# Ordering VectorE's work in bundles 1 to 3 of a convolution and channel-mix kernel, and parting one cast between ScalarE and VectorE

## Chip, cores and metric

The kernel runs on one core of a Trainium2 chip. The metric is the device time of one execution in microseconds, as the median of several runs. The core has five engines with a queue each, which meet at semaphores: TensorE (PE, matmuls), VectorE (DVE), ScalarE (ACT), GpSimd (POOL) and SyncE (SP, which here only starts transfers). Each engine works through its own instructions in the order in which the program has them.

## The reference

The input x has 8 sequences of 4160 positions and 192 channels. A causal convolution with 7 taps comes first; its taps are a softmax over `weight`, one row for each of 8 heads of 24 channels. Its result y feeds a channel mix:

```
y_prev = y shifted by one position
xk = mu_k * y + (1 - mu_k) * y_prev
xr = mu_r * y + (1 - mu_r) * y_prev
k  = relu(xk @ w_k)                  # 192 -> 1024
v  = (k * k) @ w_v                   # 1024 -> 192
r  = sigmoid(xr @ w_r)               # 192 -> 192
out = r * v
```

## The kernel before, and what sets its order

**Tiles.** Two sequences are worked on together, so there are four pairs. Positions of a pair are cut into steps of 512 (the first pair begins and ends with a step of 256). For a step, K = xk @ w_k makes 1024 rows of k for 512 positions of two sequences; a slot is one eighth of that, a PSUM tile `ps_k` of 128 x 1024 fp32. ScalarE takes it to SBUF as `k_sb` (ReLU, `k_relu`), VectorE squares it into `k2` (`k_square`), and TensorE uses `k2` for V (`v`, `v_rows`). Four slots in a row are a bundle. Slots 0 to 3 (bundle 0) belong to step 0, slots 4 to 11 (bundles 1 and 2) to step 1, slots 12 to 19 (bundles 3 and 4) to step 2. So the third step is step 2, and the second and third bundle are bundles 1 and 2.

**Mixing.** VectorE makes xk and xr of a step from the difference d = y - y_prev (`diff`, L528): three scalings by mu, one for each third of the channels (`scale`, L559), and one addition of y_prev (`add_y`, L565). xk must be there before the first slot of its step, xr before the R of that step (`r`, L642), which runs a bundle or two later.

**Convolution.** Positions are grouped; the first groups of pair 0 are made on TensorE and stay on the chip. Group 3, the fourth, is convolved by `conv_full` in bundle 2 into two PSUM tiles `ps_c`, cast to `y` by `conv_out` (L431), turned by 15 transposes in bundle 3 (`tr`, L494) and copied into `yT` by VectorE (L503). The second of the two tiles needs two casts, of 320 and of 640 elements in each partition, since its heads cross a border between thirds of the channels. Groups 4 and 5 go through `conv_tiles` (L317) from bundle 3 on.

**What sets the order.** The program is written out by hand, bundle by bundle: `bundle_first`, `bundle_second`, `bundle_third` for bundles 0 to 2 and `bundle_rest` behind them. Pieces of mixing are put into tables (`mix_a`, `mix_b`, `mix_c`, `late`) under a bundle's number by `at`, and `run` calls them at fixed places in a bundle. Every call appends to the queue of its engine, so the order of calls is the order on each engine. Two supplies of buffers tie the engines together:

- `ring`: four PSUM buffers for every kind of tile (`ps_k`, `ps_r`, `ps_v`, `ps_c`, `ps_t`). A matmul into a new tile waits until the reader of the buffer's last tile is done.
- `four`: four buffers for `k_sb`. The ReLU of slot n waits for the square of slot n - 4.

Which free buffer of the ring a tile gets is chosen when the program is built, and can change when other work moves.

In bundle 2 TensorE does K of slots 8, 9 and 10, R of step 0, V of step 0, the two tiles of group 3 and K of slot 11. In bundle 3 it does K of slots 12 and 13, the transposes of group 3, two convolution tiles of group 4, K of slot 14, R of step 1, half of a V, K of slot 15, two more tiles, and the other half of V.

Of the kernel before, what the change touches and what calls it, by code (L numbers as in the profile page):

```python
# [14 lines left out]
def kernel(  # L15
# [11 lines left out]
    nc = tc.nc  # L27
# [36 lines left out]
    for p in range(NPAIR):  # L64
# [5 lines left out]
        for L in sizes:  # L70
            ns = L * NF // STEP
# [7 lines left out]
    bundles, bundle_of = [], {}  # L79
    n = 0  # L80
# [100 lines left out]
    n = groups[0][2] * 2 * D  # L181
# [190 lines left out]
    def conv_units(g):  # L372

        return [((0, 1), (6, 7)), ((2, 3), (4, 5))]
# [39 lines left out]
        c0 = YC + groups[g][1] + b0 * BLK  # L414
        copy(out=yTs[0][:, c, c0 : c0 + (b1 - b0) * BLK], in_=o[:, 0 : (b1 - b0) * BLK])  # L415

    def conv_out(g, c, copy):

        nb = groups[g][2]
        unit = conv_units(g)[c]  # L420
        w = G * len(unit[0])
        ps = conv_ps.pop((g, c))[:BLK, :, :]
        y = ys[g][:BLK, :, :]
        parts = []
        for hs in unit:
            c0, c1 = hs[0] * G, (hs[-1] + 1) * G
            cuts = [c0] + [a for a in range(Q, D, Q) if c0 < a < c1] + [c1]
            parts.append(sorted((b - a, a - c0, a // Q * 2 * Q + a % Q) for a, b in zip(cuts, cuts[1:])))
        for (n, s0, d0), (m, s1, d1) in zip(*parts):
            assert n == m and d1 > d0  # L430
            copy(  # L431
                out=bass.AP(
                    tensor=y.tensor,
                    offset=y.offset + d0,
                    ap=[y.ap[0], [d1 - d0, 2], [2 * D, nb], [Q, 2], [1, n]],
                ),
                in_=bass.AP(
                    tensor=ps.tensor,
                    offset=ps.offset + s0,
                    ap=[ps.ap[0], [BANK + s1 - s0, 2], [2 * w, nb], [w, 2], [1, n]],  # L440
                ),
            )
# [126 lines left out]
    def k_mm(n, cs=range(NC)):  # L569


        s, j = slots[n]
        L = steps[s][2]
        xk = xks[s]
        if cs[0] == 0 and n not in k_ps:
            k_ps[n] = ring.tile([P, 2, BANK], FP32, tag="k", name="ps_k")
        ps = k_ps[n]
        nf = STEP // L

        for c in cs:  # L580
            for f in range(nf):
                fs = slice((j * nf + f) * P, (j * nf + f + 1) * P)
                for i in range(2):
                    r = slice(i * Q, (i + 1) * Q)
                    nc.tensor.matmul(  # L585
                        out=ps[:, i, f * L : (f + 1) * L],
                        lhsT=wk[r, c, fs],
                        rhs=xk[r, c, :L],
                        start=c == 0 and f == 0,
                        stop=c == NC - 1 and f == nf - 1,  # L590
                    )

    def k_relu(n):
        ps = k_ps.pop(n)
        k_sb = four.tile([P, 2 * STEP], BF16, tag="k_sb", name="k_sb")
        k_sbs[n] = k_sb
        nc.scalar.activation(out=k_sb, in_=ps.rearrange("p a b -> p (a b)"), func=AF.Relu)  # L597

    def k_square(n):
        s, j = slots[n]  # L600
        L = steps[s][2]
        k_sb = k_sbs.pop(n)
        if j == 0:
            k2s[s] = three.tile([P, NF, 2 * STEP], BF16, tag="k2", name="k2")
        nf = STEP // L
        i = k_sb
        o = k2s[s][:, j, :]
        if nf > 1:
            i = k_sb.rearrange("p (b f t) -> p f b t", b=2, f=nf)
            o = k2s[s][:, j * nf : (j + 1) * nf, 0 : 2 * L].rearrange("p f (b t) -> p f b t", b=2)  # L610
        nc.vector.tensor_tensor(out=o, in0=i, in1=i, op=ALU.mult)  # L611
# [74 lines left out]
    def v_out(s, j):  # L686
        p, t0, L, _, _ = steps[s]
        o_sb = four.tile([P, 4, D], FP32, tag="o_sb", name="o_sb")
        nc.vector.tensor_tensor(  # L689
            out=o_sb.rearrange("p (b t) d -> p b (t d)", b=2),  # L690
            in0=v_ps.pop((s, j)),
            in1=r_sbs.pop((s, j)),
            op=ALU.mult,
        )
        for st in range(2):
            c = t0 + 2 * j * P
            nc.sync.dma_start(
                out=out[2 * p + st, c : c + 2 * P, :].rearrange("(m p) d -> p m d", p=P),
                in_=o_sb[:, 2 * st : 2 * st + 2, :],
            )  # L700
# [24 lines left out]
    early, rq, rs, xt, mix_a, mix_b, mix_c, vq, late = ({} for _ in range(9))  # L725

    def at(table, b, fn, *a):
        table.setdefault(b, []).append((fn, a))

    for g, (p, base, nb, fb, on_pe) in enumerate(groups):  # L730
# [10 lines left out]
        if g in sparse:  # L741
            at(late, max(fb - 5, xs[-1] + 2), y_read, g, slice(0, 1), 2)
            at(late, fb - 2, y_read, g, slice(1, 2), 2)
            b, b1 = {6: (3, 5), 7: (9, 10), 8: (16, 17)}.get(g, (fb - 19, fb - 16))
# [16 lines left out]
    for s, (p, t0, L, n0, ns) in enumerate(steps):  # L761
        fb = first_bundle[s]
        if s == 0:
            at(mix_a, 1, mix, s, 1)
            continue
        if s == 1:
            at(mix_b, 1, scale, s, 1, 0, 1)
            at(late, 2, scale, s, 1, 2)
            at(late, 2, add_y, s, 1)
        else:  # L770
            if s == 2:
                at(mix_c, 1, diff, s)
            elif s == 4:
                at(mix_b, fb - 1, diff, s)
            else:
                at(mix_c, fb - 2, diff, s)
            at(mix_b if s == 4 else mix_a, fb - 1, scale, s, 0, 0)
            at(mix_b, fb - 1, scale, s, 0, 1, 2)
            at(mix_c, fb - 1, add_y, s, 0)
            if s == 2:  # L780
                at(mix_a, fb, scale, s, 1, 0)
                at(mix_b, fb, scale, s, 1, 1)
            else:
                at(mix_c, fb - 1, scale, s, 1, 0)
                at(mix_a, fb, scale, s, 1, 1)
            at(mix_b, fb, scale, s, 1, 2)
            at(mix_b, fb, add_y, s, 1)
        if s == LAST - 1 or s < LAST and steps[s + 1][0] > p:
            at(late, fb - 1, keep_tail, p)
    for s, j, vb in quads:  # L790
        b = vb - (s == LAST)
# [7 lines left out]
    def run(table, b, part=slice(None)):  # L799
        for fn, a in table.get(b, [])[part]:  # L800
            fn(*a)
# [165 lines left out]
    def bundle_third(b, ns):  # L967

        quad = vq[b][0]
        first, second = xt[b - 1]  # L970
        for n in bundles[b - 1][2:]:
            k_square(n)
        run(mix_a, b)
        for n in ns[:3]:
            k_mm(n)
            k_relu(n)
        k_square(ns[0])
        run(rq, b)
        run(rs, b)
        v(*quad)  # L980
        conv_full(*first)
        conv_full(*second)
        conv_out(*first, nc.scalar.copy)
        k_square(ns[1])
        run(mix_b, b)
        k_mm(ns[3])
        k_relu(ns[3])
        conv_out(*second, nc.scalar.copy)
        v_out(*quad)
        run(mix_c, b)  # L990
        run(late, b)

# [55 lines left out]
```

## Time and profile before

| what | value |
|---|---|
| median of 3 runs | 412.27 us |
| lowest and highest run | 411.48, 414.23 us |
| profiled execution, its own time | 410.83 us |
| its span (first to last instruction) | 409.0 us |
| outside of the span | 1.83 us |
| instructions | 17463 |
| granted TensorE clock, mean | 1.000 |

The profile is of one execution, taken by the hardware. Its start times count from the first instruction. A row of a timeline merges equal instructions that follow each other; what stands in brackets is how long the engine was idle before it and what ended that idle time. In a row such as `xk<-d,mu` the tile that is written stands on the left. Numbers such as `k_sb_516`, in the lists of instructions below, tell the buffers' tiles apart: `k_sb_602`, `656`, `675`, `684`, `693`, `766`, `792` and `801` belong to slots 6 to 13, `ps_k_857` to slot 14.

### The profile page before, as it was taken

The numbers are of one execution on the slowest core, as the hardware profiler recorded it, in microseconds if no ns is written. First come the engines' busy times: TensorE is split into PE (matmuls) and PEld (weight loads), VectorE is DVE, ScalarE is ACT, GpSimd is POOL, SyncE is SP. The second block draws the span as 40 slices with busy tenths as digits, with TensorE's granted clock in tenths as the row PEclk, the third lists the DMA queues.
The fourth block names the chain that finished last, engine by engine and source line by source line (L and its number), as shares of the span: only waits on it lengthen the run. The fifth ranks groups of instructions, "written<-read, shape, count | busy, mean of one in ns | idle before, by whom it ended". The sixth has DMA issues, their size and how long they took to land.

```text
span 409.0 us, 17463 instructions
## 1 busy us (share of the span) xinstructions
PE 400.1 (98%) x7695; PEld 301.4 (74%) x7696; DVE 370.7 (91%) x672; ACT 354.3 (87%) x426; POOL 57.2 (14%) x91
## 2 busy tenths in 40 slices
PE   7889999999999999999999999999999999999996
PEld 5557777777877777777777777777777778777795
DVE  5989899998999999999999999999999899999973
ACT  6889989989888989988898998889899877877781
POOL 8632202300240202004020022000000000000000
PEclk9999999999999999999999999999999999999999
DMA  9999999989399998789995997977523846221223
GB/s 148 185 202 204 189 203 208 214 241 187 92 197 265 195 209 131 156 192 197 202 160 135 234 169 133 169 192 195 128 79 94 218 123 157 81 73 46 80 79 117
DMA packets 138955, 66.23 MB, mean 162 GB/s; under 512 B 89356, under 2 KB 138880, under 8 KB 138880
## 3 DMA queue, kind: packets, MB, share of 16 engines
q1 hardware_dynamic: 95536, 48.20, 46.9%
q0 software_dynamic: 42544, 16.36, 35.1%
q8 instruction: 60, 0.98, 1.0%
q10 hardware_dynamic: 800, 0.57, 0.5%
q14 instruction: 15, 0.12, 0.1%
HBM read 33.29 MB, written 36.86 MB: 172 GB/s over the span
## 4 chain that ended last, share of the span: by engine, by line
PE 95%; DMA 2%; POOL 1%; ACT 1%; issue 0%; DVE 0%; POOLq 0%
PE ps_k L585 41%; PE ps_v L673 41%; PE ps_r L642 8%; PE ps_c L362 2%; PE ps_v L625 2%; DMA wk<-in_moe_w_k_dram 2%; ACT k_sb L597 0%; PE ps_c L317 0%; POOL wk L224 0%; POOL xb L152 0%; PE ps_t L405 0%; PE ps_c L387 0%; ACT y L431 0%; POOL tap L258 0%; DVE o_sb L709 0%
## 5 line engine op out<-in xcount | busy, mean ns | idle before, releaser
L597 ACT ACTIVATE k_sb<-ps_k 128x1024 bf16<-128x1024 f32 x260 | 253.4, 1039 | 35.4 <-PE ps_k L585 34.6
L611 DVE TENSOR_TENSOR k<-k_sb 128x1024 bf16<-128x1024 bf16 x260 | 173.5, 688 | 24.9 <-ACT k_sb L597 24.7
L585 PE MATMUL ps_k<-xk,wk 64*128 64x512 bf16 (+1 forms) x1632 | 191.6, 367 | 2.5 <-DMA wk<-in_moe_w_k_dram 1.6
L673 PE MATMUL ps_v<-wv,k 64*128 64x192 bf16 x3968 | 185.3, 243 | 0.0
L673 PEld LDWEIGHTS <-k 64*128 64x128 bf16 x3968 | 165.7, 94 | 11.8 <-issue 4.4
L585 PEld LDWEIGHTS <-wk 64*128 64x128 bf16 x1632 | 83.3, 94 | 58.9 <-DMA wk<-in_moe_w_k_dram 2.1
L689 DVE TENSOR_TENSOR o_sb<-ps_v,r_sb 128x768 f32<-128x768 f32 x64 | 60.9, 951 | 2.6 <-issue 2.4
L152 POOL DMA_DIRECT2D xb<-in_x_dram x62 | 43.5, 708 | 132.2 <-DVE xb L111 60.1
L653 ACT ACTIVATE r_sb<-ps_r 128x768 bf16<-128x768 f32 x65 | 53.5, 824 | 7.4 <-PE ps_v L673 5.1
L335 ACT CAST y<-ps_c 128x960 bf16<-128x960 f32 (+2 forms) x84 | 52.7, 710 | 0.0
L642 PEld LDWEIGHTS <-xr 64*128 64x128 bf16 x780 | 34.9, 94 | 14.5 <-issue 0.5
L642 PE MATMUL ps_r<-wr,xr 64*128 64x192 bf16 x780 | 43.3, 243 | 0.0
L559 DVE TENSOR_SCALAR xr<-d,mu 128x512 bf16<-128x512 bf16 (+1 forms) x102 | 35.4, 351 | 0.0
L559 DVE TENSOR_SCALAR xk<-d,mu 128x512 bf16<-128x512 bf16 (+1 forms) x99 | 32.6, 358 | 0.1
L528 DVE TENSOR_TENSOR d<-yT 128x1536 bf16<-128x1536 bf16 (+4 forms) x36 | 31.2, 866 | 1.1 <-ACT yT L415 1.1
L565 DVE TENSOR_TENSOR xr<-xr,yT 128x1536 bf16<-128x1536 bf16 (+1 forms) x33 | 31.1, 941 | 1.1
L565 DVE TENSOR_TENSOR xk<-xk,yT 128x1536 bf16<-128x1536 bf16 (+3 forms) x33 | 30.5, 923 | 0.1
L512 POOL COPY y_tail<-yT 128x195 bf16<-128x195 bf16 x4 | 3.1, 764 | 88.8 <-DMA yT<-y_dram 88.8
L362 PEld LDWEIGHTS <-toe 32*32 32x32 bf16 x768 | 4.9, 87 | 10.3 <-issue 8.7
L362 PE MATMUL ps_c<-xb,toe 32*32 32x240 bf16 x768 | 10.8, 266 | 0.0
L125 POOL MEMSET xb<- 32x384 bf16 x3 | 1.2, 409 | 66.6 <-DVE xb L123 66.6
L625 PE MATMUL ps_v<-wv,k 128*128 128x192 bf16 x96 | 8.4, 246 | 0.0
(60 smaller groups left out, 62.7 us busy)
## 6 DMA issues: line engine op xcount, KB each, us to landing
out_dram<-o_sb SPq DMA_DIRECT2D x128, 192.0 KB
xb<-in_x_dram POOLq DMA_DIRECT2D x52, 240.0 KB, 8.1
y_dram<-y SPq DMA_DIRECT2D x48, 195.0 KB
y_dram<-y SPq DMA_DIRECT2D x8, 210.0 KB
xb<-in_x_dram POOLq DMA_DIRECT2D x6, 228.0 KB, 5.1
xb<-in_x_dram POOLq DMA_DIRECT2D x4, 192.0 KB, 6.3
wk<-in_moe_w_k_dram POOLq DMA_DIRECT2D x4, 192.0 KB, 6.4
wv<-in_moe_w_v_dram POOLq DMA_DIRECT2D x1, 384.0 KB, 8.4
```

The costliest lines, as they stand in the source:

```text
L152: nc.gpsimd.dma_start(out=xb[q0 : q0 + rows, lo:hi, s, :], in_=bass.AP(tensor=x.tensor, offset=x.offset + (b * S + t0 + lo * step) * D, ap ...
L335: nc.scalar.copy(out=bass.AP(tensor=y.tensor, offset=y.offset + d, ap=[y.ap[0], [m * 2 * D, 2], [2 * D, m], [Q, 2], [1, b - a]],), in_=bas ...
L528: nc.vector.tensor_tensor(out=shaped(s, diffs[s][:, cs, :L]), in0=y_of(s, cs, 1), in1=y_of(s, cs, 0), op=ALU.subtract)
L559: nc.vector.tensor_scalar(out=t[:, c, :L], in0=diffs[s][:, c, :L], scalar1=mu[:, i, c : c + 1], scalar2=None, op0=ALU.mult)
L565: nc.vector.tensor_tensor(out=o, in0=o, in1=y_of(s, sl, 0), op=ALU.add)
L585: nc.tensor.matmul(out=ps[:, i, f * L : (f + 1) * L], lhsT=wk[r, c, fs], rhs=xk[r, c, :L], start=c == 0 and f == 0, stop=c == NC - 1 and f ...
L597: nc.scalar.activation(out=k_sb, in_=ps.rearrange("p a b -> p (a b)"), func=AF.Relu)
L611: nc.vector.tensor_tensor(out=o, in0=i, in1=i, op=ALU.mult)
L642: nc.tensor.matmul(out=ps[:, i, k * D : (k + 1) * D], lhsT=xr[q, c, ts], rhs=wr[q, c, :], start=c == 0, stop=c == NC - 1,)
L653: nc.scalar.activation(out=r_sbs[s, j], in_=r_ps.pop((s, j))[:, :, 0 : 2 * D], func=AF.Sigmoid)
L673: nc.tensor.matmul(out=v_ps[s, j][:, bank, k * D : (k + 1) * D], lhsT=k2s[s][q, f, t * P : (t + 1) * P], rhs=wv[q, f, :], start=half == 0 ...
L689: nc.vector.tensor_tensor(out=o_sb.rearrange("p (b t) d -> p b (t d)", b=2), in0=v_ps.pop((s, j)), in1=r_sbs.pop((s, j)), op=ALU.mult,)
```

## The change

Four things change, all in bundles 1 to 3.

- xk of step 2 (difference, three scalings, addition) is made in bundle 2 ahead of the V product, between and behind the squares of slots 6 and 7. Before, its difference stood in bundle 1, and its parts were spread over bundle 2.
- xr of step 1: all three scalings now stand at the end of bundle 2. Before, two of them stood in bundle 1.
- The squares of slots 8 and 9 and the V product (`v_out`): the V product now comes right behind xk, and the squares come behind the V product and behind both casts of group 3.
- `conv_out` takes one copy function for each cast. Of the second tile of group 3, ScalarE keeps the cast of 320 elements and VectorE makes the one of 640.

```diff
-    def conv_out(g, c, copy):
+    def conv_out(g, c, *copies):
...
-        for (n, s0, d0), (m, s1, d1) in zip(*parts):
+        for copy, (n, s0, d0), (m, s1, d1) in zip(copies, *parts):
...
         if s == 1:
-            at(mix_b, 1, scale, s, 1, 0, 1)
-            at(late, 2, scale, s, 1, 2)
+            at(late, 2, scale, s, 1, 0, 1, 2)
             at(late, 2, add_y, s, 1)
         else:
             if s == 2:
-                at(mix_c, 1, diff, s)
+                at(mix_a, 2, diff, s)
...
-            at(mix_b if s == 4 else mix_a, fb - 1, scale, s, 0, 0)
+            at(mix_b if s in (2, 4) else mix_a, fb - 1, scale, s, 0, 0)
             at(mix_b, fb - 1, scale, s, 0, 1, 2)
-            at(mix_c, fb - 1, add_y, s, 0)
+            at(mix_b if s == 2 else mix_c, fb - 1, add_y, s, 0)
...
-        for n in bundles[b - 1][2:]:
-            k_square(n)
+        k_square(bundles[b - 1][2])
         run(mix_a, b)
+        k_square(bundles[b - 1][3])
+        run(mix_b, b)
         for n in ns[:3]:
             k_mm(n)
             k_relu(n)
-        k_square(ns[0])
         run(rq, b)
         run(rs, b)
         v(*quad)
         conv_full(*first)
         conv_full(*second)
-        conv_out(*first, nc.scalar.copy)
-        k_square(ns[1])
-        run(mix_b, b)
+        conv_out(*first, nc.scalar.copy, nc.scalar.copy)
+        v_out(*quad)
         k_mm(ns[3])
         k_relu(ns[3])
-        conv_out(*second, nc.scalar.copy)
-        v_out(*quad)
+        conv_out(*second, nc.scalar.copy, nc.vector.tensor_copy)
+        k_square(ns[0])
+        k_square(ns[1])
         run(mix_c, b)
         run(late, b)
```

VectorE's queue behind the square of slot 5, before (what stands in brackets are the engines whose semaphores an instruction waits for):

```order
L559 TENSOR_SCALAR xr_659<-d_435,mu_90 128x512 x2
L528 TENSOR_TENSOR d_662<-yT_246 128x1536 [waits Activation_49]
L611 TENSOR_TENSOR k2_644<-k_sb_602 128x1024
L611 TENSOR_TENSOR k2_644<-k_sb_656 128x1024 [waits Activation_49]
L559 TENSOR_SCALAR xk_666<-d_662,mu_90 128x512 [waits DVE_49]
L611 TENSOR_TENSOR k2_644<-k_sb_675 128x1024 [waits Activation_49]
L611 TENSOR_TENSOR k2_644<-k_sb_684 128x1024 [waits Activation_49]
L559 TENSOR_SCALAR xk_666<-d_662,mu_90 128x512 x2
L689 TENSOR_TENSOR o_sb_770<-ps_v_711,r_sb_709 128x768 [waits PE_49,Activation_49]
L565 TENSOR_TENSOR xk_666<-xk_666,yT_246 128x1536 [waits DVE_49]
L559 TENSOR_SCALAR xr_659<-d_435,mu_90 128x512
L565 TENSOR_TENSOR xr_659<-xr_659,yT_246 128x1536 [waits DVE_49]
```

The same place now:

```order
L611 TENSOR_TENSOR k2_644<-k_sb_602 128x1024 [waits Activation_49]
L528 TENSOR_TENSOR d_660<-yT_246 128x1536 [waits Activation_49]
L611 TENSOR_TENSOR k2_644<-k_sb_656 128x1024 [waits Activation_49]
L559 TENSOR_SCALAR xk_663<-d_660,mu_90 128x512 [waits DVE_49]
L559 TENSOR_SCALAR xk_663<-d_660,mu_90 128x512 x2
L565 TENSOR_TENSOR xk_663<-xk_663,yT_246 128x1536 [waits DVE_49]
L689 TENSOR_TENSOR o_sb_755<-ps_v_710,r_sb_708 128x768 [waits PE_49,Activation_49]
L431 CAST y_743<-ps_c_749 120x2x5x2x32 [waits PE_49,Activation_49]
L611 TENSOR_TENSOR k2_644<-k_sb_675 128x1024
L611 TENSOR_TENSOR k2_644<-k_sb_684 128x1024
L559 TENSOR_SCALAR xr_772<-d_435,mu_90 128x512 x3
L565 TENSOR_TENSOR xr_772<-xr_772,yT_246 128x1536 [waits DVE_49]
```

The addition for xk moved ahead of the V product and of the squares of slots 8 and 9, and a cast that waits for ScalarE (`Activation`) stands ahead of these squares. The value that this cast waits for is the one that ScalarE's cast of 320 elements, from the same PSUM tile, sets when it ends.

ScalarE's queue from the cast of group 3's first tile to the ReLUs of slots 12 and 13 and the cast behind them, before:

```order
L431 CAST y_744<-ps_c_745 120x2x5x2x48 [waits PE_49]
L597 ACTIVATE k_sb_766<-ps_k_759 128x1024 [waits DVE_49,PE_49]
L431 CAST y_744<-ps_c_750 120x2x5x2x16
L431 CAST y_744<-ps_c_750 120x2x5x2x32
L597 ACTIVATE k_sb_792<-ps_k_785 128x1024 [waits DVE_49,PE_49]
L597 ACTIVATE k_sb_801<-ps_k_794 128x1024 [waits DVE_49,PE_49]
```

And now:

```order
L431 CAST y_743<-ps_c_744 120x2x5x2x48 [waits PE_49]
L597 ACTIVATE k_sb_766<-ps_k_759 128x1024 [waits DVE_49,PE_49]
L431 CAST y_743<-ps_c_749 120x2x5x2x16
L597 ACTIVATE k_sb_792<-ps_k_785 128x1024 [waits DVE_49,PE_49,Activation_49]
L597 ACTIVATE k_sb_801<-ps_k_794 128x1024 [waits DVE_49,PE_49,Activation_49]
L335 CAST y_825<-ps_c_826 128x10x2x48 [waits PE_49]
```

The cast of 640 elements left this queue; the one of 320 still stands behind the ReLU of slot 11 (`k_sb_766`). The ReLUs of slots 12 and 13 wait for VectorE, for the squares of slots 8 and 9.

TensorE's order is the same, but some of its waits are not. The end of the second convolution tile of bundle 3 and the start of slot 14, before:

```order
L317 LDWEIGHTS toe_89
L317 MATMUL ps_c_836<-xb_241,toe_89 64x10x24
L585 LDWEIGHTS wk_91 [waits DVE_49]
L585 MATMUL ps_k_857<-xk_666,wk_91 128x512 [waits PE_49]
L585 LDWEIGHTS wk_91
```

And now:

```order
L317 LDWEIGHTS toe_89
L317 MATMUL ps_c_836<-xb_241,toe_89 64x10x24
L585 LDWEIGHTS wk_91
L585 MATMUL ps_k_857<-xk_663,wk_91 128x512 [waits Activation_49]
L585 LDWEIGHTS wk_91
```

Slot 14 got another buffer of the ring: before it waited for VectorE's copies of the transposes, now for ScalarE's cast of the tile `ps_c_826`.

## The prediction

> **What bounds the kernel now.** I read the page first: the busy times and the chain of work that ended last.
>
> ```profile
> PE 400.1 (98%) x7695; PEld 301.4 (74%) x7696; DVE 370.7 (91%) x672; ACT 354.3 (87%) x426; POOL 57.2 (14%) x91
> PE 95%; DMA 2%; POOL 1%; ACT 1%; issue 0%; DVE 0%; POOLq 0%
> ```
>
> TensorE (PE) is busy for 98% of the span and holds 95% of the chain. So a change elsewhere pays only where PE waits, and costs only where it makes PE wait. The second view is the busy time by stage; the stages are the stretch that the change touches and the one behind it.
>
> ```profile
> 24.00:31.00 7.00, 5.82 (x75) 3.29 (x74) 5.93 (x13) 6.26 (x10) 2.58 (x5) 1.00 1.50 208
> 31.00:50.00 19.00, 19.00 (x350) 13.71 (x348) 17.55 (x32) 18.50 (x25) 4.53 (x7) 1.00 1.15 203
> ```
>
> Columns: stretch, length, busy us of PE, weight loads, VectorE (DVE), ScalarE (ACT), GpSimd, clock, DMA. PE is idle 7.00 - 5.82 = 1.18 us from 24 to 31, and not at all from 31 to 50. So 1.18 us is the most that the change can win, and a delay of PE that stands at 31 is made good by nothing behind it. The third view, who waited for whom, names that idle time:
>
> ```profile
> PE ps_k L585 <- DVE xk L565: 0.9, 1, 0.9
> PE ps_c L317 <- ACT k_sb L597: 0.3, 1, 0.3
> ```
>
> The change aims at the first row. The timelines of the three engines follow; all start times below are from them (columns: start, length, engine, line, operation). A merged row's length runs from its first start to its last end.
>
> ```profile
> 21.34 2.97 PE L625 MATMUL ps_v<-wv,k 128*128 128x192 bf16 x32
> 25.06 0.82 PE L585 MATMUL ps_k<-xk,wk 64*128 64x512 bf16 x6
> 26.77 1.47 PE L585 MATMUL ps_k<-xk,wk 64*128 64x512 bf16 x12 [0.89 <-DVE xk L565]
> 28.18 0.96 PE L494 MATMUL ps_t<-ident,y 120*128 120x120 bf16 x15
> 29.07 0.40 PE L317 MATMUL ps_c<-xb,toe 64*64 64x240 bf16 x8
> 29.76 0.40 PE L317 MATMUL ps_c<-xb,toe 64*64 64x240 bf16 x8 [0.29 <-ACT k_sb L597]
> 30.09 0.82 PE L585 MATMUL ps_k<-xk,wk 64*128 64x512 bf16 x6
> 30.75 0.66 PE L642 MATMUL ps_r<-wr,xr 64*128 64x192 bf16 x12
> 31.24 1.48 PE L673 MATMUL ps_v<-wv,k 64*128 64x192 bf16 x32
> 37.11 0.66 PE L642 MATMUL ps_r<-wr,xr 64*128 64x192 bf16 x12
> ```
>
> In this view: V of bundle 2, K of slot 11, K of slots 12 and 13 (which open bundle 3), 15 transposes of y, two convolution tiles, K of slot 14, R, and the first half of V; the last row is the R of bundle 4. ScalarE, with one row by form for its long cast:
>
> ```profile
> 25.92 1.02 ACT L597 ACTIVATE k_sb<-ps_k 128x1024 bf16<-128x1024 f32 x1 [0.21 <-PE ps_k L585]
> 26.84 0.42 ACT L431 CAST y<-ps_c 120x320 bf16<-120x320 f32 x1
> 27.15 0.71 ACT L431 CAST y<-ps_c 120x640 bf16<-120x640 f32 x1
> 27.73 1.97 ACT L597 ACTIVATE k_sb<-ps_k 128x1024 bf16<-128x1024 f32 x2
> 29.55 1.93 ACT L335 CAST y<-ps_c 128x960 bf16<-128x960 f32 x3
> L335 ACT CAST y<-ps_c 128x960 bf16<-128x960 f32 x2 | 2.0, 996 | 0.0
> ```
>
> These are the ReLU of slot 11, the two casts that the change parts, the ReLUs of slots 12 and 13, and the casts behind them. VectorE, with one row by form for the nearest cast that it makes today:
>
> ```profile
> 19.46 0.69 DVE L611 TENSOR_TENSOR k<-k_sb 128x1024 bf16<-128x1024 bf16 x1
> 20.84 0.94 DVE L528 TENSOR_TENSOR d<-yT 128x1536 bf16<-128x1536 bf16 x1
> 21.71 1.28 DVE L611 TENSOR_TENSOR k<-k_sb 128x1024 bf16<-128x1024 bf16 x2
> 23.18 1.28 DVE L611 TENSOR_TENSOR k<-k_sb 128x1024 bf16<-128x1024 bf16 x2
> 24.90 0.94 DVE L689 TENSOR_TENSOR o_sb<-ps_v,r_sb 128x768 f32<-128x768 f32 x1
> 25.77 0.95 DVE L565 TENSOR_TENSOR xk<-xk,yT 128x1536 bf16<-128x1536 bf16 x1
> 26.64 0.34 DVE L559 TENSOR_SCALAR xr<-d,mu 128x512 bf16<-128x512 bf16 x1
> 29.02 1.22 DVE L503 COPY yT<-ps_t 128x720 bf16<-128x720 bf16 x3 [1.03 <-PE ps_t L494]
> 30.16 1.28 DVE L611 TENSOR_TENSOR k<-k_sb 128x1024 bf16<-128x1024 bf16 x2
> 31.36 1.01 DVE L559 TENSOR_SCALAR xr<-d,mu 128x512 bf16<-128x512 bf16 x3
> 32.40 0.96 DVE L565 TENSOR_TENSOR xr<-xr,yT 128x1536 bf16<-128x1536 bf16 x1
> 33.28 1.29 DVE L611 TENSOR_TENSOR k<-k_sb 128x1024 bf16<-128x1024 bf16 x2
> 34.48 0.95 DVE L528 TENSOR_TENSOR d<-yT 128x1536 bf16<-128x1536 bf16 x1
> 35.96 0.95 DVE L689 TENSOR_TENSOR o_sb<-ps_v,r_sb 128x768 f32<-128x768 f32 x1
> L415 DVE CAST yT<-ps_t 128x480 bf16<-128x480 f32 x2 | 1.2, 650 | 0.0
> ```
>
> An operation overlaps the next one's start, so I step VectorE by the distance of starts: square 0.60 (21.71 to 22.91 for two), difference 0.87 (20.84 to 21.71), V product 0.87 (24.90 to 25.77), add 0.87 (25.77 to 26.64), three scalings 1.04 (31.36 to 32.40), the three copies 1.14 (29.02 to 30.16). From the end of one engine's work to the start of another's I take 0.05: xk ends at 25.77 + 0.95 = 26.72 and PE starts at 26.77.
>
> **Step 1, xk earlier: a win of 1.06 us where it stands.** Up to slot 5's square at 19.46 nothing moves. Then: square 6 at 20.06, difference 20.66, square 7 21.53, three scalings 22.13, add 23.17 to 24.12. So xk is there 2.6 us sooner than 26.72. The V product waits for PE's V to end (21.34 + 2.97 = 24.31): 24.36 to 25.30, which also frees the PSUM buffer of slot 12. PE is through with issuing slot 11 at 25.06 + 0.65 = 25.71 (30.09 to 30.75 is the same six pairs) and goes on at once: 25.71 against 26.77. The 0.9 us wait is gone.
>
> **Step 2, the half cast: VectorE stands for 2.08 us.** In the new order VectorE's cast waits for ScalarE, for the other half of the same cast. That half sits behind the ReLU of slot 11, which waits for PE, and PE's slot 11 is not earlier than before. So it still runs from 26.84 to 27.26, and VectorE, free at 24.36 + 0.87 = 25.23, starts the cast at 27.31. The trace has no such cast on VectorE: below it is the 0.65 us cast of 480 elements, above it the 0.94 us product of 768 out of PSUM. In proportion to the 640 elements I take 0.81 and keep both ends: 28.12. Behind it in VectorE's queue stand the squares of slots 8 and 9, which before ran at 23.18: now 28.04 to 28.72 and 28.64 to 29.32.
>
> [...] The rows at 26.84 and 27.15 show the two halves overlapping by 0.11 us on one engine, and from these rows alone one might hope that two engines can share them. [...]
>
> **Step 3, who waits for the squares.** The ReLU output has four buffers, so slot 12's ReLU needs slot 8's square: it starts at 28.77 instead of 27.73, and the 0.71 us that ScalarE was relieved of is lost in this wait. Slots 12 and 13 end at 29.82 and 28.77 + 1.97 = 30.74. PE, early by 1.06, meanwhile transposes: it starts at 27.31, waits at the third one for VectorE's half (28.17), and has the other 13 out by 28.17 + 13/15 of 0.89 = 28.94. Then it stands. The two convolution tiles take the PSUM buffers of slots 12 and 13: 29.87 and 30.79, against 29.07 and 29.76. Slot 14 now takes the buffer of the first of these tiles, so it waits for its cast (two ReLUs later, 28.77 + 1.82 = 30.59, and 1.00 long): 31.64 against 30.09, plus 1.55 us. R follows at 32.30, V at 32.79.
>
> **Step 4, xr and the squares of slots 10 and 11.** VectorE after 28.64: scalings at 29.24 (xr of step 1, all three now here), add 30.28 to 31.23 (in time for R), the small memset 31.15, the copies 31.21 (the two that R's buffer needs are done by 32.2), squares 32.35 and 32.95 to 33.63. V reads slot 11's square after 14 of its 32 matmuls, 14/32 of 1.32 (30.75 + 0.49 to its successor), so at 32.79 + 0.58 = 33.37. It waits to 33.68: 0.31 more, together 1.86. The two chains agree: even if slot 14 had kept its old buffer, VectorE would hold V until 33.68, and 33.68 - 31.82 is 1.86.
>
> **Step 5, bundle 4.** VectorE from 33.55: 1.04 + 0.87 for xr of step 2, 1.20 for two squares, 0.87 difference, 0.60 square: the V product at 38.13 to 39.08 instead of 35.96. R of bundle 4 needs its buffer; PE comes there at 37.11 + 1.86 = 38.97 and goes on at 39.13: 0.16 more. Sum: 1.55 + 0.31 + 0.16 = 2.02, so 2.0 us later. Behind that VectorE has 19.00 - 17.55 = 1.45 us of room up to 50 and catches up, PE has none.
>
> **Costed at nothing.** The V product is 0.54 us earlier, and so are its two output transfers on SP; nothing is queued near them. The memset that frees GpSimd's loads of group 6 is 3.2 us later:
>
> ```profile
> 28.13 0.41 POOL L125 MEMSET xb<- 32x384 bf16 x1 [5.19 <-DVE xb L123]
> 58.21 0.56 PE ps_c L362 x32
> ```
>
> Their first reader comes at 58.21, some 27 us after the later memset; that cover holds unless they took more than that.
>
> **The rivals.** *The wait goes and nothing takes its place.* The 0.89 us row speaks for it. It would be 412.27 - 0.9 = 411.4, not slower. It is decided by the start of VectorE's cast: the square of slot 8 must be done by about 27.15, when ScalarE is free for slot 12, so the cast must start by about 25.7; and slot 14 would have to keep its old buffer. Against it: the other half ends at 27.26, and the buffer has changed. Chance 0.05.
>
> *The halves run side by side.* VectorE casts from 25.28, slot 12's ReLU starts at 27.20 (ScalarE's own order), 0.53 us earlier; but slot 14 then waits for 27.20 + 1.82 + 1.00 + 0.05 = 30.07 against 30.09. The early start of PE is eaten by the buffer's hand-over and the time stays 412.3. Against it: the wait in the order. Chance 0.09.
>
> *More than the sum.* VectorE, 2.2 us late with 91% load, could hold up PE in later bundles as in step 5: 0.16 in each of eight more would give 1.3, so 415.6. For it: only 1.45 us of room in 19. Against: that room is enough after two or three bundles. Chance 0.10.
>
> **How the numbers follow.** The profiled execution took 410.83 us (span 409.0); it becomes 412.8. The median of the three runs shown is 412.27, 1.44 above it, and with the same 2.0 it becomes 414.3. That is the forecast, chance 0.76: slower by 0.5%. Its own range is 0.16 less to 0.13 more from the cast, and about 1 us either way from the runs, which lie between 411.48 and 414.23: 413.1 to 415.4. Taking in most of the two cases near 412.3 and the case of 415.6 gives 412.0 to 416.4; the first rival is left out. About 1% (4.1 us) is what a measurement of this kernel can tell from no change. Slower by over 1% would need 2.1 us beyond the sum, where the third rival has 1.3 (0.04); faster by over 1% is excluded by the 1.18 us of idle time but for a disturbed median (0.01); within 1%: 0.95.
>
> **What would show it.** Right: PE's wait for xk gone and slot 12 at about 25.7; a wait of some 2 us on VectorE ahead of a cast at L431, ended by ScalarE's cast; slot 12's ReLU waiting about 1.6 us for a square; PE waiting for ReLUs and casts for about 3.5 us in all between 27 and 34. Wrong: VectorE's cast starting before 26, or PE at R of bundle 4 by 37.2 or sooner.

## The result, and the profile after

| | before | after |
|---|---|---|
| median | 412.07 us (16 runs, 410.85 to 414.41) | 414.92 us (16 runs, 413.18 to 418.47) |
| ratio | | 1.0069, 95% interval 1.0051 to 1.0088 |
| profiled execution | 410.83 us, span 409.0 | 416.49 us, span 414.8 |

The changed kernel is 2.85 us slower, 0.7%. The forecast was 414.3 us, 2.0 us slower, with a range of 412.0 to 416.4. The profiled execution of after is one of its slower ones: its span is 5.8 us longer, of which 1.3 us is a wait for `xb` at 62 us (see the loads of group 6) and 0.8 us a wait for ScalarE at 140 us that no other trace has. So the stretch of the change is compared by itself and not by the spans. It is measured from the first matmul of group 3's convolution (L387) to R of bundle 4 (L642). Before, that is 24.15 to 37.11, 12.96 us; only its first row has not been shown yet:

```profile
24.15 0.98 PE L387 MATMUL ps_c<-xb,toe 128*128 128x240 bf16 x8
```

The timeline of TensorE after (columns as in the prediction):

```profile
24.42 0.98 PE L387 MATMUL ps_c<-xb,toe 128*128 128x240 bf16 x8
25.34 2.12 PE L585 MATMUL ps_k<-xk,wk 64*128 64x512 bf16 x18
...
28.46 0.86 PE L494 MATMUL ps_t<-ident,y 120*128 120x120 bf16 x13 [0.58 <-DVE y L431]
30.19 0.40 PE L317 MATMUL ps_c<-xb,toe 64*64 64x240 bf16 x8 [0.87 <-ACT k_sb L597]
31.10 0.62 PE L317 MATMUL ps_c<-xb,toe 64*64 64x240 bf16 x8 [0.52 <-ACT k_sb L597]
31.95 1.47 PE L585 MATMUL ps_k<-xk,wk 64*128 64x512 bf16 x6 [0.23 <-ACT y L335]
33.19 1.19 PE L642 MATMUL ps_r<-wr,xr 64*128 64x192 bf16 x12
34.15 1.58 PE L673 MATMUL ps_v<-wv,k 64*128 64x192 bf16 x32
...
40.11 0.66 PE L642 MATMUL ps_r<-wr,xr 64*128 64x192 bf16 x12
```

From 24.42 to 40.11 are 15.69 us: 2.73 more than before, nearly all of the 2.85. The 0.89 us in front of slot 12 is gone (18 matmuls in one piece from 25.34), and four waits stand behind it. The list of TensorE's waits from 24 to 50 us (engine, tile and line, whom it waited for: us in all, times, longest):

```profile
PE ps_c L317 <- ACT k_sb L597: 1.4, 2, 0.9
PE ps_t L494 <- DVE y L431: 0.6, 1, 0.6
PE ps_k L585 <- ACT y L335: 0.2, 1, 0.2
```

That is 2.2 us in place of the 1.2 of before. In the timeline comes, besides, something that the prediction does not have: slot 14's six pairs take 33.19 - 31.95 = 1.24 us where they took 0.66, and R takes 34.15 - 33.19 = 0.96 where it took 0.49. VectorE and ScalarE:

```profile
24.69 0.96 DVE L689 TENSOR_TENSOR o_sb<-ps_v,r_sb 128x768 f32<-128x768 f32 x1 [0.26 <-PE ps_v L625]
27.57 0.82 DVE L431 CAST y<-ps_c 120x640 bf16<-120x640 f32 x1 [1.92 <-ACT y L431]
28.32 1.28 DVE L611 TENSOR_TENSOR k<-k_sb 128x1024 bf16<-128x1024 bf16 x2
```

```profile
27.12 0.42 ACT L431 CAST y<-ps_c 120x320 bf16<-120x320 f32 x1
29.11 1.94 ACT L597 ACTIVATE k_sb<-ps_k 128x1024 bf16<-128x1024 f32 x2 [1.57 <-DVE k L611]
```

VectorE stands for 1.92 us ahead of its half of the cast, until ScalarE's half has ended; the squares of slots 8 and 9 come at 28.32, and ScalarE then stands for 1.57 us for the first of them. Last, busy times by stretch of 3.41 us (length, busy PE, weight loads, VectorE, ScalarE, GpSimd, clock, DMA):

```profile
27.48:30.90 3.42, 1.53 (x23) 1.11 (x24) 3.29 (x7) 1.85 (x3) 0.00 (x0) 1.00 1.43 216
30.90:34.31 3.41, 2.97 (x29) 1.89 (x30) 3.41 (x9) 2.73 (x5) 2.46 (x5) 0.50 0.29 54
34.31:37.72 3.41, 3.41 (x78) 2.69 (x75) 3.38 (x7) 2.18 (x4) 1.84 (x3) 1.00 1.25 135
```

The granted clock is 0.50 from 30.90 to 34.31, which holds the two long rows (31.95 to 34.15), and 1.00 on both sides. Before, it was 1.00 through this whole stretch. In the stretch just ahead, TensorE was busy for only 1.53 of 3.42 us, since the waits add up there, though none of them is longer than 0.9 us.

### The profile page after: what moved, and what is told of

Its sections match the earlier page's. It is cut to its first block, busy times and chain, and to the rows that moved or that the text cites. A ratio compares the mean times of both kernels' runs of the same rounds, so it can differ in the third digit from the quotient of the medians.

```text
span 414.8 us, 17464 instructions
## 1 busy us (share of the span) xinstructions
PE 403.3 (97%) x7695; PEld 304.2 (73%) x7696; DVE 372.2 (90%) x673; ACT 354.3 (85%) x425; POOL 58.2 (14%) x91
## 4 chain that ended last, share of the span: by engine, by line
PE 80%; DMA 5%; ACT 1%; SPq 1%; issue 0%; DVE 0%; ACTq 0%
PE ps_v L673 36%; PE ps_k L585 34%; PE ps_r L642 7%; DMA xb<-in_x_dram 3%; PE ps_c L362 2%; DMA y_dram<-y 2%; PE ps_v L625 1%; SPq L458 1%; ACT y L335 1%; ACT k_sb L597 0%; DVE o_sb L709 0%; ACTq L335 0%
## 5 line engine op out<-in xcount | busy, mean ns | idle before, releaser
L642 PEld LDWEIGHTS <-xr 64*128 64x128 bf16 x780 | 35.3, 95 | 14.7 <-issue 0.9
L642 PE MATMUL ps_r<-wr,xr 64*128 64x192 bf16 x780 | 43.8, 245 | 0.0
L512 POOL COPY y_tail<-yT 128x195 bf16<-128x195 bf16 x4 | 4.0, 1004 | 87.8 <-DMA yT<-y_dram 87.8
L362 PEld LDWEIGHTS <-toe 32*32 32x32 bf16 x768 | 5.0, 87 | 11.9 <-issue 9.0
L362 PE MATMUL ps_c<-xb,toe 32*32 32x240 bf16 x768 | 11.1, 267 | 1.4 <-DMA xb<-in_x_dram 1.3
```

The costliest lines, as they stand in the source:

```text
L642: nc.tensor.matmul(out=ps[:, i, k * D : (k + 1) * D], lhsT=xr[q, c, ts], rhs=wr[q, c, :], start=c == 0, stop=c == NC - 1,)
```

## The experiments

The theory (A): nearly all of the loss comes from one wait, VectorE's for ScalarE's half; the squares behind it hold up the ReLUs, and these the convolution tiles and slot 14. Against it stand three rivals: the moves of xk and of the V product do harm by themselves; the early xk pays as soon as the wait is gone; a part of the cast on VectorE costs what it takes there, wherever it stands. For the rest, the half clock, theory F holds that it follows from TensorE's idle time. The verdicts below name the rivals in words. The differences of the stretch below are against the 12.96 us of before.

**All of the cast on ScalarE, the rest of the change kept.**

```diff
-        conv_out(*second, nc.scalar.copy, nc.vector.tensor_copy)
+        conv_out(*second, nc.scalar.copy, nc.scalar.copy)
```

> The changed kernel with one part undone: both casts of group 3's second tile stay on ScalarE. Theory A (the loss comes from VectorE's queue, where the cast stands for 1.9 us and holds up the squares of slots 8 and 9): no wait of VectorE ahead of these squares, slot 12's ReLU starts right behind the casts as in the kernel before, R of bundle 4 comes as early as before, and the time is that of the kernel before, 412.1 (411.4 to 412.8), since the early xk only moves PE's wait from slot 12 to the two convolution tiles. Theory B (the new order of xk, the V product, the squares and xr costs by itself): 1 us or more of the 2.8 us stays, 413.1 or above. Theory C (xk's wait of 0.9 us was worth its length): 411.2, below the kernel before.

Measured: 412.1 us (12 runs, 410.48 to 415.96), ratio 1.0001 (0.9978 to 1.0025). TensorE's timeline:

```profile
24.74 0.98 PE L387 MATMUL ps_c<-xb,toe 128*128 128x240 bf16 x8
25.65 2.12 PE L585 MATMUL ps_k<-xk,wk 64*128 64x512 bf16 x18
...
28.51 0.86 PE L494 MATMUL ps_t<-ident,y 120*128 120x120 bf16 x13 [0.32 <-ACT y L431]
...
30.35 0.40 PE L317 MATMUL ps_c<-xb,toe 64*64 64x240 bf16 x8 [0.52 <-ACT k_sb L597]
30.68 0.82 PE L585 MATMUL ps_k<-xk,wk 64*128 64x512 bf16 x6
```

R of bundle 4 is at 37.70: 12.96 us, a difference of 0.00. The whole loss hangs on VectorE's half. And the early xk buys nothing by itself: slot 12 still starts without a wait, but TensorE now waits for ScalarE's casts and ReLUs, which were never early. Theory A stands. That the moves do harm by themselves falls, and that the early xk pays without the wait falls for this form.

**VectorE's half first.** VectorE casts its 640 elements as soon as the tile is there, and ScalarE its 320 behind that.

```diff
-        conv_out(*second, nc.scalar.copy, nc.vector.tensor_copy)
+        conv_out(*second, nc.vector.tensor_copy, nc.scalar.copy, last_first=True)
...
+        if last_first:
+            parts = [part[::-1] for part in parts]
```

> The changed kernel with the two halves of the cast in the other order: VectorE's 640 elements first, ScalarE's 320 behind them, so that ScalarE waits for VectorE and not the other way round. Theory A: VectorE starts its cast right behind the V product (about 25.5), squares of slots 8 and 9 are done by 27.5, slot 12's ReLU starts at about 27.3, R of bundle 4 comes within 0.3 us of the kernel before, 412.2 in all. Theory D (a cast of this size on VectorE costs by its 0.82 us of VectorE's time, wherever it stands): R of bundle 4 is 0.8 us later than before, 412.9 or more. Theory C: 411.2.

Measured: 412.9 us (12 runs, 410.81 to 416.94), ratio 1.003 (1.0 to 1.006). VectorE, then TensorE:

```profile
26.71 0.82 DVE L433 CAST y<-ps_c 120x640 bf16<-120x640 f32 x1
27.44 1.29 DVE L613 TENSOR_TENSOR k<-k_sb 128x1024 bf16<-128x1024 bf16 x2
```

```profile
31.46 0.82 PE L587 MATMUL ps_k<-xk,wk 64*128 64x512 bf16 x6 [0.48 <-DVE yT L505]
```

The cast has no wait, and the stretch takes 12.92 us (25.57 to 38.49): 0.04 less than before. What harmed was not that VectorE makes a part of the cast, as the third rival has it, but that it makes the second part. The relief of ScalarE is eaten too: VectorE is now late with the copies of the transposes, which slot 14 needs. The time is unclear, between the same and 0.6% slower, and by the time alone (412.9 or more was expected of it) the third rival could stand; it is the stretch that speaks against it. What the 0.3% are is not shown: the mean clock of the profiled execution is 0.996, though R takes 0.66 to 0.67 us and 18 matmuls of K 2.11 to 2.12 wherever they stand between 17 and 70 us, as at full clock, and TensorE has a wait of 0.9 us for `xb` behind the stretch.

**The squares ahead of the cast.** The cast stays parted as in the change, but the squares of slots 8 and 9 stand ahead of VectorE's half.

```diff
-        conv_out(*second, nc.scalar.copy, nc.vector.tensor_copy)
         k_square(ns[0])
         k_square(ns[1])
+        conv_out(*second, nc.scalar.copy, nc.vector.tensor_copy)
```

> The changed kernel with the squares of slots 8 and 9 ahead of VectorE's half of the cast; the halves keep their order, so VectorE still waits for ScalarE, with the squares done. Theory A: slot 12's ReLU is on time (about 27.3) and PE does not wait for ReLUs longer than before; what is left is that xr, the copies of the transposes and the squares of slots 10 and 11 come behind the waiting cast: R of bundle 4 about 1.0 us later than before, 413.1 in all. Theory E (the transposes, which wait for VectorE's half, are what costs, and the squares matter little): as the changed kernel, 414.9.

Measured: 413.47 us (12 runs, 412.0 to 416.78), ratio 1.0038 (1.0016 to 1.0061). VectorE, then TensorE:

```profile
27.12 1.28 DVE L611 TENSOR_TENSOR k<-k_sb 128x1024 bf16<-128x1024 bf16 x2
29.13 0.82 DVE L431 CAST y<-ps_c 120x640 bf16<-120x640 f32 x1 [0.72 <-ACT y L431]
```

```profile
32.69 0.82 PE L585 MATMUL ps_k<-xk,wk 64*128 64x512 bf16 x6 [1.29 <-DVE yT L503]
```

The wait is 0.72 us in place of 1.92, since two squares now fill it. The chain through the ReLUs is gone; the late VectorE now reaches slot 14 by its copies. The stretch takes 13.74 us, 0.78 more than before (1.0 was expected), with the clock at 1.00. So of the 2.73 us the larger part hangs on the place of that wait, as theory A has it.

**The gaps filled.** The changed kernel, with 42 transposes that nobody reads in TensorE's gaps of bundle 3: repeats among the transposes of y, and 14, 8 and 10 around the convolution tiles. Slot 14's buffer waits for VectorE's copies in this kernel.

```diff
+    def busy(g, t, n):
+        for _ in range(n):
+            nc.tensor.transpose(out=t[:, 1, 0:BLK], in_=ys[g][:BLK, 0, 0:P], identity=ident[:BLK, :BLK])
...
+            def tiles(spare):
+                busy(3, spare, 14)
+                for u, n in zip(xt[b - 1], (8, 10)):
+                    conv_tiles(*u)
+                    busy(3, spare, n)
+                    conv_tiles_out(*u)
```

> The changed kernel with 42 added transposes on TensorE, in the places where it waits in bundle 3 (ten repeat the first two transposes of y, the others write a half of a PSUM tile that nothing reads). Their results are not used; slot 14 gets its PSUM buffer from VectorE's copies instead of ScalarE's cast. The waits on VectorE and ScalarE stay. Theory F (part of the loss is TensorE's clock, which stood at half for 3.4 us from 30.9 because TensorE had been idle for much of the time before): the clock stays at 1.0 from about 10 us to the end, K of slot 14 takes 0.65 us and R 0.49 us from start to start, V of bundle 3 ends about 0.8 us earlier than in the changed kernel, and the time is 414.1. Theory G (the clock falls for another reason, or costs nothing): half clock in this stage as before, or no gain at the end of V, 414.9 or more, by what the added transposes cost.

Measured: 413.93 us (7 runs, 413.27 to 414.99), ratio 1.0038 (1.001 to 1.0066). Busy times by stretch, at the same place as the first two above:

```profile
26.88:30.29 3.41, 3.07 (x51) 2.31 (x47) 2.83 (x7) 1.84 (x4) 0.00 (x0) 1.00 1.51 212
30.29:33.70 3.41, 3.21 (x62) 2.32 (x56) 3.41 (x8) 3.00 (x5) 2.00 (x4) 1.00 0.52 97
```

VectorE waits as long as in the changed kernel, the same 1.92 us, but TensorE is busy for 3.07 us of the stretch, and the clock stays at 1.00. From 24.28 to 39.21 are 14.93 us: 1.97 more than before and 0.76 less than after. Adding work made this stretch shorter. The medians go the same way, but the intervals of the two ratios (1.001 to 1.0066, and 1.0051 to 1.0088) overlap. Theory F holds: in this kernel the waits cost 1.97 us, and the half clock 0.76. Since slot 14 waits for another buffer here, the split need not be the same in the changed kernel; a trace of it at full clock, shown with the loads of group 6, has 1.86 and 0.87.

**A part of the gaps filled.** The same without the 8 and 10 transposes at the two tiles.

```diff
-                for u, n in zip(xt[b - 1], (8, 10)):
+                for u in xt[b - 1]:
                     conv_tiles(*u)
-                    busy(3, spare, n)
                     conv_tiles_out(*u)
```

> The changed kernel with 24 of the 42 filling transposes: those among the transposes of y and the 14 ahead of the first convolution tile stay, the 18 behind the two tiles are left out. The fill changes no output. Theory F (the granted clock halves for one step of 3.41 us after a step in which TensorE was busy for less than about 2 us): the step that holds the gaps is now at 2.4 us or more wherever it begins, so the clock stays at 1.0 there as with all 42: mean clock 0.998 or more in most runs and a median of 413.9 (413.4 to 414.5). Rival G (what counts is any gap of half a microsecond, of which the last two are open again): half clock in most runs as in the changed kernel, mean clock 0.996 or less, and 414.7 to 415.

Measured: 414.22 us (12 runs, 413.06 to 416.66), ratio 1.0041 (1.002 to 1.0061); the mean clock is 0.998 or more in 10 of the 12 runs, where it is 0.996 or less in 13 of the 16 of the changed kernel, and in 9 of 64 of the kernel before. The mean does not tell where the half clock stood: the profiled execution here is one of the two others, and its half clock comes behind a wait of 1.6 us for `xb`: 18 matmuls of K take 3.47 us at 64.11 and 2.11 before it. From the lengths of these rows it begins at about 63.5, an estimate. TensorE, and the busy times of the step of 3.41 us that holds the gaps (ten such steps ahead of that half clock):

```profile
30.92 0.40 PE L317 MATMUL ps_c<-xb,toe 64*64 64x240 bf16 x8 [0.52 <-ACT k_sb L603]
32.16 0.82 PE L591 MATMUL ps_k<-xk,wk 64*128 64x512 bf16 x6 [0.83 <-DVE yT L505]
```

```profile
29.32:32.73 3.41, 1.92 (x33) 1.14 (x32) 3.38 (x10) 3.33 (x5) 1.06 (x3) 1.00 0.67 146
```

Two gaps of 0.52 and 0.83 us are open again, and the six pairs behind them still take 0.82 us at full clock. The stretch takes 14.94 us (24.24 to 39.18), as with all gaps filled. TensorE is busy for 1.92 us of that step, less than the 2.4 us that was expected, and the clock stays at 1.00 in it and in the next (R takes 0.66 us there, at 32.81). So gaps of 0.52 and 0.83 us were not enough here, and rival G falls. The busy time over some 3.4 us fits (1.53 us of work ahead of a clock of 0.50 in the changed kernel, 1.92 us ahead of 1.00 here), but the "less than about 2 us" of theory F was the author's estimate, and no run shows where such a border would lie.

**The short part first, on VectorE.** The cast is parted the other way round: VectorE takes the 320 elements and comes first, ScalarE keeps the 640.

```diff
-        conv_out(*second, nc.scalar.copy, nc.vector.tensor_copy)
+        conv_out(*second, nc.vector.tensor_copy, nc.scalar.copy)
```

> The cast is parted the other way round: VectorE takes the short half (320 elements a partition) and comes first, ScalarE keeps the long one (640) behind the ReLU of slot 11. Theory A (the loss of the changed kernel is VectorE standing for ScalarE's half, and what hangs on the squares behind it): VectorE casts with no wait at about 26, the squares follow at once, R of bundle 4 is 0.0 to 0.1 us later than in the kernel before, and the time is that of the kernel before, 412.2 (411.8 to 412.9). Rival B (any part of this cast on VectorE costs what it takes there, since VectorE is the bound of this stretch): 0.4 us more, 412.6, with a wait of PE on VectorE's copies of the transposes ahead of slot 14. Rival D (the early xk pays once ScalarE is relieved without a wait, here of 0.3 us): R of bundle 4 0.3 to 0.9 us sooner and 411.3 to 411.9.

Measured: 411.69 us (12 runs, 410.61 to 412.83), ratio 0.9977 (0.9956 to 0.9999). VectorE, then TensorE:

```profile
25.11 0.96 DVE L689 TENSOR_TENSOR o_sb<-ps_v,r_sb 128x768 f32<-128x768 f32 x1 [0.25 <-PE ps_v L625]
25.99 0.48 DVE L431 CAST y<-ps_c 120x320 bf16<-120x320 f32 x1
26.39 1.28 DVE L611 TENSOR_TENSOR k<-k_sb 128x1024 bf16<-128x1024 bf16 x2
```

```profile
28.28 0.86 PE L494 MATMUL ps_t<-ident,y 120*128 120x120 bf16 x13 [0.20 <-ACT y L431]
...
30.12 0.40 PE L317 MATMUL ps_c<-xb,toe 64*64 64x240 bf16 x8 [0.52 <-ACT k_sb L597]
30.46 0.82 PE L585 MATMUL ps_k<-xk,wk 64*128 64x512 bf16 x6
```

From 24.84 to 37.48 are 12.64 us, 0.32 less than before. Here the early xk pays at last, because ScalarE is relieved of 0.3 us and nobody waits for it: the second rival holds for this form, if for no more than the lower end of what it was given. It beats both kernels by its median, though its interval ends at 0.9999: a win of some tenths of a us that is just on the edge of what can be told.

**The loads of group 6.** The profiled execution of after also lost 1.3 us at 62, in a wait for `xb`, and other traces of changed kernels did as well:

```profile
62.74 0.38 PE L362 MATMUL ps_c<-xb,toe 32*32 32x240 bf16 x20 [1.29 <-DMA xb<-in_x_dram]
```

So the kernel before was run again for a second trace.

> The kernel before, unchanged, for a second trace of it. If the late transfers of group 6 (TensorE waiting 1.3 us for xb at about 62 us in the profiled execution of the changed kernel) belong to the change, no such wait stands here; if they come and go with the run, it may. From the first convolution of group 4 to R of bundle 4 all theories expect 12.96 us as in the first trace (12.9 to 13.0), and a clock of 1.0 from 24 to 50.

It took 411.49 us (one run), the stretch again 12.96 us (24.60 to 37.56), with no wait of TensorE for `xb` in the list. These are the rows of the tile `xb` from 44 to 60 us, on the issue of group 6's second batch of loads and on its time to landing, of before and of after:

```profile
L152 POOL DMA_DIRECT2D xb<-in_x_dram x4: 678/683/723, 45.7 to 47.8; - x4
DMA to landing us min/median/max: 6.4/7.5/10.5
```

```profile
L152 POOL DMA_DIRECT2D xb<-in_x_dram x4: 676/681/721, 48.5 to 50.5; - x4
DMA to landing us min/median/max: 7.5/8.9/12.2
```

In before, the last load is issued at 47.8 and lands, if the longest time is its own, 10.5 us later, at 58.3; group 6's convolution (L362) starts at 58.1. In the second trace of before it is 48.2, 10.7 and 58.9, with a start at 58.6. There is no cover at all, in either trace of before. Over all nine traces of this layout the longest of these loads took 10.5 to 13.3 us, and TensorE waited for 0 to 2.5 us. Would it help to issue these loads a bundle earlier? The same edit was made to the changed kernel, to the kernel before, and to the one with the short part first:

```diff
-            b, b1 = {6: (3, 5), 7: (9, 10), 8: (16, 17)}.get(g, (fb - 19, fb - 16))
+            b, b1 = {6: (3, 4), 7: (9, 10), 8: (16, 17)}.get(g, (fb - 19, fb - 16))
```

> The changed kernel, with the second batch of group 6's loads (and the small VectorE memset that orders it) one bundle earlier, in bundle 4 in place of 5. The last of these loads lands in every trace so far within some 2 us of the first matmul that reads it (about 58 to 62 us), so it has no cover, though the prediction gave it 27 us. Theory H (the wait for it comes and goes with the run and is no part of the difference between the two kernels): no wait of TensorE for xb at about 60, the last load lands 5 us or more ahead of its reader; R of bundle 4 is still 2.0 (clock full) to 2.8 us (one half-clock step) later than before; the median falls by 0.3 to 1 us against 414.9, to 413.9 to 414.6, and the slowest runs come down most. Theory I (the wait is part of what the change costs): the median falls by 1.3 us or more, to 413.6 or below, and more than the kernel before does by the same edit. Rival J (the earlier loads collide with the transposing loads of y in bundle 4): those end later, TensorE waits for yT before step 2, and nothing is won.

> The kernel before with the same edit: group 6's second batch one bundle earlier. Its two traces show that load landing 0.2 and 0.1 us ahead of its reader, with no wait to speak of; of its 53 runs some were 3 us and more slower than the rest. Theory H: those late runs go, the median falls by 0 to 0.5 us, to 411.7 to 412.4. Theory I: the median stays within 0.2 us of that of the kernel before. Rival J: slower by 0.5 us or more, with a wait for yT.

> The kernel with VectorE's short half first (411.69 us, 0.23% under the kernel before) with the same edit of the loads: if both parts hold, R of bundle 4 is 0.3 us sooner than in the kernel before, no wait of 0.6 us for xb stands at about 59, and the median is 411.0 to 411.6. Rival K (the 0.23% was chance): 412 or more.

Measured: 420.69 us (6 runs, ratio 1.0212, 1.0174 to 1.0251), 417.56 us (6 runs, 1.0139, 1.0107 to 1.0171) and 418.13 us (4 runs, 1.0139, 1.0107 to 1.0171). All three went the way of rival J, which says what to look for: the queue of SP, of before and of before with earlier loads.

```profile
41.38 3.88 SPq L480 DMA_TRANSPOSE yT<-y_dram  x2
```

```profile
41.12 10.11 SPq L480 DMA_TRANSPOSE yT<-y_dram  x2
```

The two transposing loads of y, 3.88 us before, take 10.11 us beside the loads of `xb`; TensorE then waits for xk of a later step, which is made from them: 1.3 us at 56.9 here, and 3.0 and 4.5 us in the other two kernels. (The trace here is of the fastest of its six runs, 414.82 us, so it shows the kind of the loss and not all of it.) So these loads can't go there, and the 0.2% of the short part first can't be widened in this way. Whether the late loads have a share in the 2.85 us stays open: they come and go with the run, the two traces of before have no such wait, and five of the seven traces of other kernels with the loads in their old place do, but the first experiment, whose trace has the longest (2.5 us), has the median of before. With the loads earlier the two kernels still lie 420.69 - 417.56 = 3.1 us apart.

The trace of the changed kernel with the earlier loads shows one thing more. The edit first acts at 42.0 us, behind the stretch, so up to R of bundle 4 this is the changed kernel itself, with the same buffers and no added work; but the steps of 3.41 us begin elsewhere in it: one at 26.83, 2.09 us behind the first matmul of the stretch, where one of after begins 3.06 us behind it (27.48 and 24.42). The 26.83 is an estimate, ten steps ahead of this trace's own half clock, in which 18 matmuls of K take 3.80 us at 60.87 in place of 2.11. TensorE, and the two steps over which the waits are spread:

```profile
24.74 0.98 PE L387 MATMUL ps_c<-xb,toe 128*128 128x240 bf16 x8
32.27 0.82 PE L585 MATMUL ps_k<-xk,wk 64*128 64x512 bf16 x6 [0.45 <-ACT y L335]
33.41 1.61 PE L673 MATMUL ps_v<-wv,k 64*128 64x192 bf16 x32
34.86 0.81 PE L585 MATMUL ps_k<-xk,wk 64*128 64x512 bf16 x6
39.56 0.67 PE L642 MATMUL ps_r<-wr,xr 64*128 64x192 bf16 x12
```

```profile
26.83:30.25 3.42, 2.08 (x25) 1.12 (x22) 2.36 (x5) 1.85 (x3) 0.00 (x0) 1.00 1.54 213
30.25:33.66 3.41, 2.18 (x40) 1.51 (x41) 3.38 (x9) 3.00 (x6) 1.50 (x3) 1.00 0.43 93
```

The waits are those of the profiled execution of after, none is filled, and the clock stays at 1.00. The stretch takes 14.82 us (24.74 to 39.56): 1.86 more than before, a little less than the 2.0 that was expected for full clock, and 0.87 less than at half clock. So in the changed kernel the waits cost 1.86 us and the half clock 0.87.

## Why the prediction came out as it did

The whole stretch of after lies 24.42 - 24.15 = 0.27 us later by its start-up, which is taken off here from every time.

**Step 1, right.** Slot 12 follows slot 11 at once: 25.34 + 0.65 - 0.27 = 25.72, where 25.71 was forecast. The wait for xk is gone.

**Step 2, right.** The wait is 1.92 us against 2.08: the cast starts at 27.30 (27.31), takes 0.82 us (0.81), and the squares start at 28.05 (28.04). The wait is counted from the end of the V product, 25.38; the forecast counted from 25.23, one step of 0.87 behind its start. The second rival, the halves side by side, falls by this row: VectorE is free and stands until ScalarE has done. Here the wait is the one that the program has, VectorE's cast waiting for ScalarE's, and it took 1.92 us; whether the halves of one tile could run side by side without it, no run shows.

**Step 3, right.** ReLU of slot 12 at 28.84 (28.77), convolution tiles at 29.92 and 30.83 (29.87, 30.79), slot 14 at 31.68 (31.64). The list of waits has 2.2 us for it, where about 3.5 were named to be seen: it was too high, the times themselves are not.

**Steps 4 and 5, right in kind, one too long.** In the profiled execution of after, V shows no wait for the square and R of bundle 4 none for the V product, because TensorE came late to both: it ran at half clock until 34.31. The trace of the changed kernel at full clock (the one with the loads earlier, taken back by 24.74 - 24.15 = 0.59 us) shows both. Slot 14 is at 31.68 there too. V takes 34.86 - 33.41 = 1.45 us to its successor where it took 1.32, so 0.13 more in place of 0.31, since the second of the two squares ended at 33.45, not 33.63. From there to R of bundle 4 are 39.56 - 34.86 = 4.70 us, where 37.11 - 32.56 = 4.55 were (32.56 is V's start, 31.24, with its 1.32), so 0.15 more in place of 0.16. In all 1.86 us were measured where the steps made 2.02. In the two filled kernels slot 14 waits for VectorE's copies, as in the kernel before, and they lose 1.97 and 1.98 us: the change of the buffer is not what costs, as the prediction said of its two chains.

**The term that was missing** is the clock. The prediction's sum took every matmul behind the waits at full clock. Measured from the same rows, slot 14 took 1.24 - 0.66 = 0.58 and R 0.96 - 0.49 = 0.47 us more; about 0.1 followed at the start of V. Of these 1.1 us some 0.28 (0.13 + 0.15) lies where steps 4 and 5 have TensorE wait anyway. That leaves about 0.85, and 0.87 was measured between the two traces. With it the forecast would have been 412.27 + 2.0 + 0.87 = 415.1; 414.92 was measured. That the time came as near as 0.6 us without it is in part luck: the kernel before had 412.07 over 16 runs, 0.2 less than the forecast began from, and the steps were 0.16 too long. In the trace at full clock the steps of 3.41 us begin elsewhere: the idle time is parted between two of them (2.08 and 2.18 us of work, where one step of after has 1.53), and the half clock stayed away. This fits the 3 of 16 runs with a mean clock above 0.996.

**Costed at nothing, wrong in its reason.** The 27 us of cover for group 6 were counted from the first batch of loads. The second batch is issued at 45.7 and has none. Its share in the result could not be told from the spread between runs.

**The third rival** (more than the sum, 415.6) named the wrong mechanism: behind bundle 4 TensorE does not wait for VectorE again, to the end of the trace.

## What to carry to other kernels

When a copy is parted between two engines, look at what the second part waits for: here the part given to the free engine stood behind a part on a busy one for 1.92 us, freed nobody, and every instruction behind it in that queue inherited the wait. Part it so that the early engine goes first, and with the short part if that engine has work behind it (0.32 us of the stretch here, at the edge of what the times can tell). And add up TensorE's short waits over a few us before taking the work behind them at full clock: here 1.53 us of work in 3.42 stood ahead of a clock of 0.50, at which slot 14 took 1.24 us in place of 0.66 and R 0.96 in place of 0.49.

## What the runs showed of the hardware

**Half clock without a long gap.** In the profiled execution of after the clock of TensorE stood at 0.50 for 3.41 us (30.90 to 34.31) and at 1.00 on both sides. In the 3.42 us just ahead TensorE had 1.53 us of work, with no wait over 0.9 us. The longest case, the kernel with the short part first and earlier loads:

```profile
52.75:56.16 3.41, 1.25 (x32) 1.02 (x26) 1.60 (x4) 1.13 (x2) 0.00 (x0) 1.00 1.28 237
56.16:59.57 3.41, 1.04 (x6) 0.42 (x8) 3.41 (x7) 0.00 (x0) 0.00 (x0) 0.50 0.81 232
59.57:62.98 3.41, 3.41 (x22) 1.48 (x20) 3.38 (x7) 2.43 (x3) 0.00 (x0) 0.50 0.50 158
```

One wait of 4.5 us stands ahead of two steps at half clock, the second of them with TensorE busy throughout: 0.50 came behind 1.25 and behind 1.04 us of work. In the other steps shown above, 1.00 came behind 1.92 us (a part of the gaps filled), 2.08 us (the changed kernel with earlier loads, with the same waits parted over two steps) and 3.07 us (the gaps filled). Whether the busy time alone decides, and where a border would lie, no run shows.

**Transposes that nobody reads kept the clock up**: the step with the waits had 3.07 us of work in place of 1.53, the next one stood at 1.00 in place of 0.50, and the stretch took 14.93 against 15.69 us.

**Transposing loads beside others** were slowed: with the loads of `xb` a bundle earlier, the two of y took 10.1 to 12.0 us, in three traces, in place of 3.7 to 5.3 in the other nine, and TensorE waited 1.3 to 4.5 us for the xk that is made from them. The longest load of `xb` that the changed kernel issued from 43.8 us on took 13.2 us there, within the 10.5 to 13.3 of the other nine traces.
